# State @ w_in as float32r products of split parts, with later stores, a step on GpSimd and another order of the first steps

## The chip, the cores and the metric

One core of one Trainium2 chip runs the whole program. The metric is the device time of one execution in microseconds; of several runs of the same kernel the median counts. TensorE is called PE here, VectorE DVE, ScalarE ACT, GpSimd POOL and SyncE SP, as in the profile.

## What is computed

A small attention between tokens and a state (8 batches, 8 heads, 512 tokens, 32 state rows, head width 64) is followed by two feed-forward layers. All inputs and outputs are float32.

```python
scores = scale * (x @ state.T);  a  = softmax(scores);   xread = a @ state
scores2 = scale * (state @ x.T); a2 = softmax(scores2);  sread = a2 @ x
x = concat([xread, sread], axis=tokens)          # 8 x 544 rows of 512
h = x @ w_in                                     # 512 -> 2048
y = maximum(0.01 * h, h) @ w_out                 # 2048 -> 512
out = (silu(y @ w_gate) * (y @ w_val)) @ w_out2  # 512 -> 1536 -> 512
```

The weights arrive as pairs of 32-bit words (they are float64) and the kernel makes float32 numbers of them itself.

## The kernel before

**The three-pass product.** Where the kernel wants float32 accuracy it splits an operand into a high part (float32r, a cast on ACT, `split_h`, line 164) and a low part (the difference, on DVE, `split_l`, line 167), and multiplies low by high, high by low and high by high: three matmuls of 128x512 (`passes`, line 436). Nearly all of the program is made of these.

**State times w_in.** For the token rows xread is a @ state, so x @ w_in = a @ (state @ w_in). The kernel therefore forms state @ w_in (called sw) once, for each of four column groups g of w_in. This is done in two ways, both with plain float32 operands. `state_win` (line 453) makes what batch 0 needs, from a block layout `states` of the state, and keeps it on the chip; its two matmuls write 64 rows each. `product_sw` (line 462) makes the rows of four batches at once, for one pair of heads p: two matmuls, e = 0 and 1, one on partitions 0 to 63 and one on 64 to 127, into two PSUM banks. ACT copies both banks to a staging tile (line 474), and SP stores them to `sw_dram` (line 477), from where later batches load them (`load_sw`, line 504). There are 32 such products (4 groups, 4 pairs, 2 halves of the batches), listed in `products`; `pump_products` (line 1213) takes the next one whose weights are ready. Its banks are two of the y banks in the first steps, and a and b, always the same two, later. Five sets of staging tiles are used in turn (`stage_sw`, line 481).

**Making the weights.** `convert` (line 234) is a generator that a caller advances one quarter step at a time. For each 128x512 tile (a key) it issues on ACT a scale (line 214) and a conversion of the low word (line 215), and on DVE the sign (line 216), the limit (line 219, min and max against a constant), a join (line 222) and an add (line 225). Two keys are in work at a time, one behind the other, and the keys of w_out ("out") get their split into high and low parts a step after that. The 32 keys of the first layer are 16 of w_in ("in") and 16 of w_out, in the order of the string `ORDER`. The loads come on SP's queue (line 197) into five buffers; the finished w_in tiles are also stored to DRAM for later use (line 232), on the same queue.

**The order of the work.** It is written out by hand. `LOADS` orders the first DMAs. `START` is a string of letters for the first steps: c advances `convert` by a quarter of a key, p makes a product, 0 and 1 advance the attention of batch 0 (scores, softmax steps and splits, `read_state`, line 304) for its two quads of heads, h and l make and split a `state_win`, s and S lay out the state for the first and for the other batches, m makes the first h. The 16 strings of `SLOT0` then do the same for the 16 slots of batch 0: H makes h (six matmuls) for two slots later, Y and Z make y (two times six matmuls) from the activated h of this slot. Each engine gets its instructions in just this order and works them off in order. After batch 0 the later slots (1.36 us of h and 2.72 us of y each) have no products or weights of the first layer between them.

Of the kernel before, what the change touches and what calls it, by code (L numbers as in the profile page):

```python
# [25 lines left out]
def kernel(  # L26
# [38 lines left out]
    nc = tc.nc  # L65
# [25 lines left out]
    START = "spc0Scpccc0p0cpccpcc1ccchcc1cccpc1clcpp0hcccpclp1c01cpcmcc"  # L91
# [116 lines left out]
    def to_f32(key):  # L208
# [3 lines left out]
        v = raw[key].bitcast(I32)  # L212
        return {
# [5 lines left out]
            "limit": lambda: nc.vector.tensor_scalar(  # L219
# [14 lines left out]
    def convert(keys, room, prepare, load_next, finish=None):  # L234
# [4 lines left out]
        while todo or before or (finish and done):  # L239
# [209 lines left out]
    WO = {}  # L449
    products = []  # L450
    sw_ps, SW_raw, SW = {}, {}, {}
# [26 lines left out]

    sw_stages = []

    def stage_sw():

        if not sw_stages:
            y, x = ab.tile([P, KD, S], F32, tag="yst", name="sw"), first1.tile([P, 2, 512], F32, tag="x_tail", name="sw")
            sw_stages[:] = [[y[:, 0], y[:, 1]], [y[:, 2], y[:, 3]], [x[:, 0], x[:, 1]]] + [
# [18 lines left out]
    def load_sw(b, g, q):  # L504
        assert not any((g, p, b // 4) in products for p in (2 * q, 2 * q + 1))
        t = SW_raw[b, g, q] = xin.tile([P, 512], F32, tag="sw", name="sw")
# [525 lines left out]
    with tc.manual_schedule():  # L1032
# [15 lines left out]
        pair = [None]  # L1048

        def place1(key):  # L1050

            if key[0] == "in":
                n, half = divmod(KD * key[1] + key[2], 2)
                if half == 0:
# [438 lines left out]
```

## Time and profile before

| | |
|---|---|
| median of three runs | 1471.44 us (1468.38 to 1471.83) |
| the profiled execution: its own time | 1469.83 us |
| its span | 1468.0 us, 20651 instructions |
| busy: PE / DVE / ACT / POOL | 1444.3 / 829.5 / 687.8 / 3.0 us |
| DMA | 307.55 MB, mean 209 GB/s |

The span is cut into 40 slices on the page; the first four slices (some 147 us) hold the first steps and batch 0's slots, which is where the changed code runs. The granted clock stands at full speed in nearly all of the rest. A busy engine is one with an instruction in it; PE's matmuls overlap each other, so the distance from one start to the next is what a matmul costs.

### The profile page before, as it was taken

To read this page: it belongs to the slowest core of one execution; us is meant where nothing else is said; L and a number is where in the kernel's file an instruction comes from. 1 tells how busy PE (TensorE), PEld (TensorE's weight loads), DVE (VectorE), ACT (ScalarE), POOL (GpSimd) and SP (SyncE) were. 2 spreads that over 40 slices of the span, in tenths; PEclk is the share of its full clock that TensorE was granted. 3 is DMA by queue.
4 is the path that set the end of the run, shared out by engine and by line. 5 is a ranking of instruction groups with operands and counts; after the bars stand their busy time and mean duration, and the time that the engine had idled before them with its cause. 6 is when DMAs were issued, how large, how long until landed. Compare 5 with 4: busy or idle time off the path is not lost.

```text
span 1468.0 us, 20651 instructions
## 1 busy us (share of the span) xinstructions
PE 1444.3 (98%) x7530; PEld 1153.4 (79%) x7530; DVE 829.5 (57%) x1476; ACT 687.8 (47%) x1243; POOL 3.0 (0%) x8
## 2 busy tenths in 40 slices
PE   6999999999999999999999999999999999999998
PEld 1545777777777778888888888888888888988887
DVE  5877677677767676243454535555344655544442
ACT  6877656655655665454333433334233343333322
POOL 0000000000000000000000000000000000000000
PEclk8999999999999999999999999999999999999999
DMA  8895556665655656360668676667666397876345
GB/s 283 301 319 200 187 198 228 204 222 197 233 204 194 224 194 208 97 198 35 203 199 277 232 235 199 194 220 243 231 193 194 101 321 241 267 251 192 116 153 191
DMA packets 145764, 307.55 MB, mean 209 GB/s; under 512 B 14080, under 2 KB 34816, under 8 KB 144640
## 3 DMA queue, kind: packets, MB, share of 16 engines
q1 hardware_dynamic: 144368, 297.72, 61.7%
q10 hardware_dynamic: 1296, 8.52, 1.4%
q8 instruction: 60, 0.98, 0.3%
q14 instruction: 40, 0.33, 0.1%
HBM read 231.74 MB, written 74.45 MB: 209 GB/s over the span
## 4 chain that ended last, share of the span: by engine, by line
PE 97%; ACT 1%; DVE 1%; DMA 0%; issue 0%; SPq 0%; ACTq 0%
PE ps_y L444 24%; PE ps_o L444 19%; PE ps_x L742 18%; PE ps_h L444 14%; PE ps_s L742 9%; PE ps_a L742 4%; PE ps_sw L468 2%; PE ps_t L444 2%; PE ps_yt L444 2%; PE ps_s L319 1%; PE ps_r L416 1%; PE ps_sw L456 1%; PE ps_a L402 0%; ACT sw L474 0%; DMA flat<-in_dram 0%
## 5 line engine op out<-in xcount | busy, mean ns | idle before, releaser
L444 PE MATMUL ps_y<-gh,w_parts 128*128 128x512 f32 x1024 | 339.3, 391 | 0.0
L742 PE MATMUL ps_x<-yc,wq 128*128 128x512 f32 x1152 | 278.0, 389 | 0.0
L742 PEld LDWEIGHTS ps_x<-yc,wq 128*128 128x128 f32 x1152 | 216.2, 188 | 44.8
L444 PE MATMUL ps_o<-wo,zh 128*128 128x512 f32 x768 | 236.3, 389 | 0.0
L444 PEld LDWEIGHTS ps_y<-gh,w_parts 128*128 128x128 f32 x1024 | 192.2, 188 | 51.7 <-issue 7.6
L444 PE MATMUL ps_y<-gl,w_parts 128*128 128x512 f32 x512 | 199.4, 389 | 0.0
L168 DVE TENSOR_TENSOR gl<-hs,gh 128x512 fp32r<-128x512 f32 (+1 forms) x144 | 95.1, 661 | 141.6 <-ACT gh L165 141.4
L444 PEld LDWEIGHTS ps_o<-wo,zh 128*128 128x128 f32 x768 | 144.2, 188 | 29.8
L550 ACT ACTIVATE hs<-ps_h 128x512 f32<-128x512 f32 (+1 forms) x144 | 82.7, 574 | 172.4 <-PE ps_h L444 168.8
L444 PE MATMUL ps_o<-wo,zl 128*128 128x512 f32 x384 | 149.5, 389 | 0.1
L742 PE MATMUL ps_s<-yc,wq 128*128 128x512 f32 x576 | 146.1, 389 | 0.0
L168 DVE TENSOR_TENSOR zl<-z,zh 128x512 fp32r<-128x512 f32 x96 | 66.4, 691 | 114.6 <-ACT zh L165 114.6
L742 PEld LDWEIGHTS ps_s<-yc,wq 128*128 128x128 f32 x576 | 108.1, 188 | 22.4
L165 ACT CAST zh<-z 128x512 fp32r<-128x512 f32 x96 | 59.3, 622 | 140.7 <-PE ps_o L444 140.6
L762 ACT ACTIVATE sg<-C 128x512 f32<-128x512 f32 x72 | 45.5, 632 | 158.1 <-DVE C L758 158.1
L444 PEld LDWEIGHTS ps_y<-gl,w_parts 128*128 128x128 f32 x512 | 96.1, 188 | 19.6
L444 PE MATMUL ps_h<-ah,swl 128*128 128x512 f32 x256 | 106.3, 415 | 1.1 <-DVE swl L168 1.1
L758 DVE TENSOR_TENSOR C<-ps_s,C 128x512 f32<-128x512 f32 x48 | 33.2, 691 | 122.9 <-PE ps_s L742 122.9
L444 PE MATMUL ps_h<-al,swh 128*128 128x512 f32 x256 | 100.2, 391 | 0.2 <-DVE al L168 0.2
L754 ACT COPY C<-ps_x 128x512 f32<-128x512 f32 x96 | 55.9, 583 | 94.6 <-PE ps_x L742 94.6
L444 PE MATMUL ps_h<-ah,swh 128*128 128x512 f32 x256 | 100.2, 391 | 0.0
L165 ACT CAST gh<-hs 128x512 fp32r<-128x512 f32 (+1 forms) x144 | 85.7, 595 | 3.0
(129 smaller groups left out, 1912.8 us busy)
## 6 DMA issues: line engine op xcount, KB each, us to landing
wo<-wo SPq DMA_DIRECT2D x96, 512.0 KB
wq<-quad_gate SPq DMA_DIRECT2D x168, 256.0 KB
wq<-quad_val SPq DMA_DIRECT2D x168, 256.0 KB
ws<-in_dram SPq DMA_DIRECT2D x68, 512.0 KB
sw<-sw_dram SPq DMA_DIRECT2D x56, 256.0 KB
quad_gate<-hl SPq DMA_DIRECT2D x24, 512.0 KB
quad_val<-hl SPq DMA_DIRECT2D x24, 512.0 KB
yr<-y_dram SPq DMA_DIRECT2D x34, 256.0 KB
```

Source lines behind the costliest of these rows:

```text
L165: nc.scalar.copy(dst, src)
L168: nc.vector.tensor_tensor(out=dst, in0=src, in1=hi.bitcast(F32), op=ALU.subtract)
L319: nc.tensor.matmul(ps[2 * NS * i:2 * NS * (i + 1)], lhsT=states[:, p, b, :], rhs=xt.pop((b, p)), start=True, stop=True,)
L416: nc.tensor.matmul(ps[NS * k:NS * (k + 1), i], lhsT=v["et"][:, n:n + NS], rhs=tokens[i][:, c, NS * k:NS * (k + 1)], start=(c == 0), stop=( ...
L444: nc.tensor.matmul(ps, lhsT=w, rhs=v, start=first and n == 0, stop=last and n == len(todo) - 1)
L456: nc.tensor.matmul(ps[2 * NS * i:2 * NS * (i + 1)], lhsT=states[:, 2 * q + i, b, :], rhs=raw["in", g, 2 * q + i], start=True, stop=True,)
L468: nc.tensor.matmul(ps[e], lhsT=flat[half, p, 4 * bs:4 * bs + 4, :].rearrange("d b n -> d (b n)"), rhs=raw["in", g, p][half], start=True, s ...
L550: nc.scalar.activation(hs, ps[:, :n], AF.Prelu, alpha=0.01)
L742: nc.tensor.matmul(bank, lhsT=a, rhs=v, start=first and n == 0, stop=last and n == len(todo) - 1, skip_group_check=True,)
L754: nc.scalar.copy(t[0], src)
L758: nc.vector.tensor_tensor(out=kept[0], in0=bank, in1=kept[0], op=ALU.add)
L762: nc.scalar.activation(t[0], c, AF.Sigmoid)
```

## The change

- `product_sw` and `state_win` work on split parts: the state is split once (`flat_h`, `flat_l`, and for batch 0 a block layout `firsts_hl`), every w_in key is split like the w_out keys into a tile of `wres` (`finish1_h`, `finish1_l`), and three float32r passes take the place of one float32 product. `state_win` now multiplies full 128x128 blocks by `passes`, six matmuls instead of two. A w_in key is ready for products after its split, one step of `convert` later than before.
- the stores of a product are issued by `store_sw`, called when the next product is made (or before a load that needs them); there are four sets of staging tiles instead of five, and `flat` moves to another pool.
- `limit` runs on GpSimd for all keys but the first four.
- the layout of the state for batches 1 to 7 moves from ACT to GpSimd, which also fills `firsts_hl` by 16 small copies; ACT's table is loaded by a copy that waits for no DMA.
- `START` is rewritten: 28 quarter steps instead of 30, eight letters p instead of eleven (seven products are made ahead of the first y in both). `SLOT0` is as it was.

```diff
-    START = "spc0Scpccc0p0cpccpcc1ccchcc1cccpc1clcpp0hcccpclp1c01cpcmcc"
+    START = "sccccScc0ccc0cpccc10cpccpc1cpc0chc1chpc0lcp1l1mcpcpcc"
...
+        engine = nc.gpsimd if key[0] in ("in", "out") and key not in keys1[:4] else nc.vector
-            "limit": lambda: nc.vector.tensor_scalar(
+            "limit": lambda: engine.tensor_scalar(
...
-                if not finish or before[0] == "in":
+                store(before)
+                if not finish:
                     ready.append(before)
-                    store(before)
...
-    def state_win(b, g, q, bank):
+    def state_win(g, q, bank):
         ps = (ps_y if bank == "y" else ps_a).tile([P, 512], F32, tag=bank, name="ps_sw")
-        for i in range(2):
-            nc.tensor.matmul(
-                ps[2 * NS * i:2 * NS * (i + 1)], lhsT=states[:, 2 * q + i, b, :], rhs=raw["in", g, 2 * q + i],
-                start=True, stop=True,
-            )
+        passes(
+            [((first_h[:, 2 * q + i], first_l[:, 2 * q + i]), WIN[g, 2 * q + i]) for i in range(2)], ps, True, True
+        )
...
-        for e in range(2):
-            half = slice(D * e, D * (e + 1))
-            nc.tensor.matmul(
-                ps[e], lhsT=flat[half, p, 4 * bs:4 * bs + 4, :].rearrange("d b n -> d (b n)"),
-                rhs=raw["in", g, p][half], start=True, stop=True,
-            )
+        wh, wl = WIN[g, p]
+        for n, (st, w) in enumerate(((flat_l, wh), (flat_h, wl), (flat_h, wh))):
+            for e in range(2):
+                half = slice(D * e, D * (e + 1))
+                nc.tensor.matmul(
+                    ps[e], lhsT=st[half, p, 4 * bs:4 * bs + 4, :].rearrange("d b n -> d (b n)"), rhs=w[half],
+                    start=n == 0, stop=n == 2,
+                )
         staged = stage_sw()
         for e in range(2):
             nc.scalar.copy(staged[e], ps[e])
-            r = slice(NS, P) if bs == 0 else slice(0, P)
-            nc.sync.dma_start(out=sw_dram[bs][g][2 * p + e, r], in_=staged[e][r])
+        store_sw()
+        unstored.append((g, p, bs, staged))
...
         def finish1_h(key):
-            while any((KD * g + p) // 2 + NF1 // 2 == key[1] for g, p, _ in products):
-                pump_products(1)
-            t = wres.tile([P, 2, 512], F32R, tag=f"wr{key[1]}", name="w_parts")
+            place = key[1] if key[0] == "out" else places[KD * key[1] + key[2]]
+            clear(place)
+            t = wres.tile([P, 2, 512], F32R, tag=f"wr{place}", name="w_parts")
...
+        table = cv.tile([P, 1], F32, name="table")
+        nc.gpsimd.memset(table, 0.0)
+        nc.scalar.copy(table, table)
...
+        def split_states():
+            split_h(flat_h, flat)
+            split_l(flat_l, flat, flat_h)
+            for t, of in ((first_h, flat_h), (first_l, flat_l)):
+                for p in range(NPAIR):
+                    for e in range(2):
+                        half = slice(D * e, D * e + D)
+                        c = NS * (2 * (p % 2) + e)
+                        nc.gpsimd.tensor_copy(out=t[half, p, c:c + NS], in_=of[half, p, 0])
...
             elif action == "S":
-                place_states(slice(1, B))
+                split_states()
+                place_states(slice(1, B), nc.gpsimd.tensor_copy)
```

Three places show how this moves instructions. The first is PE in the first steps. Before, from the first scores (`ps_s`) to the first h (`ps_h`); `ps_sw<-w_in,flat` are products (x2 is one product), `ps_sw<-w_in,states` is a `state_win`:

```order
L319 MATMUL ps_s<-xt,states 64x512 x2
L468 MATMUL ps_sw<-w_in,flat 128x512 x2
L319 MATMUL ps_s<-xt,states 64x512 x2
L456 MATMUL ps_sw<-w_in,states 64x512 x2
L468 MATMUL ps_sw<-w_in,flat 128x512 x6
L456 MATMUL ps_sw<-w_in,states 64x512 x2
L468 MATMUL ps_sw<-w_in,flat 128x512 x6
L444 MATMUL ps_h<-ah,swl 128x512
```

Now, from the third product on (a product is two matmuls with `flat_l` and four with `flat_h`; `firsts_hl` x12 are both `state_win`):

```order
L474 MATMUL ps_sw<-w_parts,flat_l 128x512 x2
L474 MATMUL ps_sw<-w_parts,flat_h 128x512 x4
L446 MATMUL ps_sw<-w_parts,firsts_hl 128x512 x12
L474 MATMUL ps_sw<-w_parts,flat_l 128x512 x2
L474 MATMUL ps_sw<-w_parts,flat_h 128x512 x4
L474 MATMUL ps_sw<-w_parts,flat_l 128x512 x2
L474 MATMUL ps_sw<-w_parts,flat_h 128x512 x4
L446 MATMUL ps_h<-ah,swl 128x512
```

Seven products stood ahead of the first h; now five do, and the sixth and seventh stand between the first h and the second.

The second place is ACT a little before that first h. Before (214 and 215 are the scale and low-word steps of `convert`, `sw<-ps_sw` the copies of products, `ah` the splits of the two quads' softmax):

```order
L165 CAST ah<-a_298 128x512
L165 CAST swh<-ps_sw 128x512
L215 ACTIVATE ws<-ws 128x512
L474 COPY sw<-ps_sw 128x512 x2
L214 ACTIVATE ws<-ws 128x512
L165 CAST w_parts<-raw 128x512
L474 COPY sw<-ps_sw 128x512 x2
L165 CAST ah<-a_341 128x512
```

Now (216 and 217 are the same two steps):

```order
L165 CAST ah<-a_318 128x512
L165 CAST swh<-ps_sw 128x512
L216 ACTIVATE ws<-ws 128x512
L165 CAST w_parts<-raw 128x512
L346 ACTIVATE st<-st 128x512
L217 ACTIVATE ws<-ws 128x512
L165 CAST swh<-ps_sw 128x512
L480 COPY sw<-ps_sw 128x512 x2
L216 ACTIVATE ws<-ws 128x512
L165 CAST w_parts<-raw 128x512
L217 ACTIVATE ws<-ws 128x512
```

Casts of weight keys have come in, and the scale of the seventh key (the second 216) stands behind the cast of the second `state_win` and the copies of the fourth product.

The third place is DVE at the same time, from the steps that follow the first quad's softmax to the low split `al` of the second quad. Before:

```order
L168 TENSOR_TENSOR swl<-ps_sw,swh 128x512
L350 TENSOR_REDUCE r_336<-st 128x16
L351 TENSOR_SCALAR r_336<-r_336 128x16
L352 RECIPROCAL r_336<-r_336 128x16
L353 TENSOR_TENSOR st<-st,r_336 128x512
L355 STREAM_TRANSPOSE a_341<-st 128x512
L216 TENSOR_SCALAR w_in<-ws 128x512
L168 TENSOR_TENSOR al<-a_298,ah 128x512
L168 TENSOR_TENSOR al<-a_341,ah 128x512
```

Now:

```order
L168 TENSOR_TENSOR swl<-ps_sw,swh 128x512
L218 TENSOR_SCALAR raw<-ws 128x512
L352 TENSOR_REDUCE r_395<-st 128x16
L353 TENSOR_SCALAR r_395<-r_395 128x16
L354 RECIPROCAL r_395<-r_395 128x16
L355 TENSOR_TENSOR st<-st,r_395 128x512
L357 STREAM_TRANSPOSE a_400<-st 128x512
L168 TENSOR_TENSOR swl<-ps_sw,swh 128x512
L168 TENSOR_TENSOR al<-a_400,ah 128x512
```

The sign step of the seventh key (216, now 218), which reads what ACT's scale of that key wrote, has moved from behind the second quad's softmax steps to ahead of them.

## Rows read from the trace of the kernel before

**Rows 1.** The page, part 1: busy time, share of the span and instructions of each engine.

```profile
PE 1444.3 (98%) x7530; PEld 1153.4 (79%) x7530; DVE 829.5 (57%) x1476; ACT 687.8 (47%) x1243; POOL 3.0 (0%) x8
```

**Rows 2.** Stretches: length, busy PE, PEld, DVE, ACT, POOL (instructions), clock, DMA share, GB/s.

```profile
38.29:133.09 94.80, 90.25 (x336) 47.93 (x335) 77.42 (x147) 79.73 (x148) 0.00 (x0) 1.00 0.87 291
68.46:76.56 8.10, 8.10 (x31) 4.16 (x32) 7.63 (x16) 8.08 (x15) 0.00 (x0) 1.00 0.95 304
139.00:159.00 20.00, 20.00 (x90) 16.56 (x89) 6.29 (x11) 10.41 (x20) 0.00 (x0) 1.00 0.61 184
```

**Rows 3.** PE's waits, then ACT's, in 38 to 140 us: total, times, longest.

```profile
PE ps_sw L468 <- ACT sw L474: 3.5, 5, 0.8
...
ACT sw L474 <- PE ps_sw L468: 5.8, 12, 0.7
ACT swh L165 <- PE ps_sw L456: 5.1, 4, 2.1
...
ACT ws L214 <- DMA ws<-in_dram: 0.9, 2, 0.7
```

**Rows 4.** PE in order of time, one product between y and h: start, duration.

```profile
129.91 0.40 PE L444 MATMUL ps_y<-gh,w_parts 128*128 128x512 f32 x1
130.24 1.13 PE L468 MATMUL ps_sw<-w_in,flat 64*128 64x512 f32 x4
131.29 0.50 PE L444 MATMUL ps_h<-ah,swl 128*128 128x512 f32 x1
131.63 0.39 PE L444 MATMUL ps_h<-al,swh 128*128 128x512 f32 x1
131.86 0.39 PE L444 MATMUL ps_h<-ah,swh 128*128 128x512 f32 x1
```

**Rows 5.** The chain that ended last, two products in a row and a state_win: start, length.

```profile
110.77 1.11 PE ps_sw L468 x4
111.88 0.57 ACT sw L474
...
112.50 1.61 PE ps_sw L468 x3
...
117.05 1.01 PE ps_sw L456 x4
```

**Rows 6.** Groups of instructions of ACT and DVE, 0 to 140 us: busy, mean ns, idle before.

```profile
L474 ACT COPY sw<-ps_sw 128x512 f32<-128x512 f32 x64 | 34.5, 591 | 10.3 <-PE ps_sw L468 10.2
L165 ACT CAST w_parts<-raw 128x512 fp32r<-128x512 f32 x16 | 9.9, 618 | 0.0
...
L219 DVE TENSOR_SCALAR ws<-ws 128x512 f32<-128x512 f32 x32 | 13.5, 423 | 0.0
L168 DVE TENSOR_TENSOR w_parts<-raw,w_parts 128x512 fp32r<-128x512 f32 x16 | 10.9, 684 | 0.0
```

**Rows 7.** First steps: stretches (as rows 2), ACT in order of time, the chain.

```profile
7.80:20.00 12.20, 6.75 (x14) 1.52 (x12) 6.03 (x11) 7.33 (x13) 0.00 (x0) 0.72 0.66 238
20.00:36.00 16.00, 13.95 (x33) 4.38 (x31) 15.58 (x31) 11.71 (x22) 0.00 (x0) 0.79 0.95 328
28.00:32.00 4.00, 4.00 (x10) 0.81 (x9) 3.86 (x9) 2.58 (x5) 0.00 (x0) 0.50 1.00 356
...
4.85 1.28 ACT L1239 ACT_TABLE_LOAD   x1 [4.85 <-DMA flat<-in_dram]
10.27 1.88 ACT L1239 COPY states<-flat 64x896 f32<-64x896 f32 x2
...
37.51 3.51 PE ps_h L444 x14
```

**Rows 8.** Groups of POOL, whole span (as rows 6); SP's longest wait, 0:140.

```profile
L1350 POOL MEMSET zero<- 128x512 f32 x1 | 0.5, 526 | 548.9 <-PE ps_r L416 548.9
masks.py:199 POOL TENSOR_SCALAR_AFFINE_SELECT ident<-ident 128x128 f32<-128x128 f32 x1 | 0.3, 292 | 0.1
...
SPq L477 <- ACT sw L474: 35.2, 25, 3.8
```

More of the change, by code (lines that the diff above doesn't have):

```diff
@@ L449 @@
     WO = {}
+    WIN = {}
     products = []
+    kept = set()
     sw_ps, SW_raw, SW = {}, {}, {}
-    def state_win(b, g, q, bank):
+    def state_win(g, q, bank):
         ps = (ps_y if bank == "y" else ps_a).tile([P, 512], F32, tag=bank, name="ps_sw")
-        for i in range(2):
-            nc.tensor.matmul(
-                ps[2 * NS * i:2 * NS * (i + 1)], lhsT=states[:, 2 * q + i, b, :], rhs=raw["in", g, 2 * q + i],
-                start=True, stop=True,
-            )
+        passes(
+            [((first_h[:, 2 * q + i], first_l[:, 2 * q + i]), WIN[g, 2 * q + i]) for i in range(2)], ps, True, True
+        )
+        kept.add((g, q))
         return ps
@@ L505, in load_sw @@
         assert not any((g, p, b // 4) in products for p in (2 * q, 2 * q + 1))
+        if any((g, p, b // 4) == one[:3] for one in unstored for p in (2 * q, 2 * q + 1)):
+            store_sw()
         t = SW_raw[b, g, q] = xin.tile([P, 512], F32, tag="sw", name="sw")
@@ L1046, in next_load1, with clear, finish1_h @@
                 stage(key, src, cv)
-        pair = [None]
         def place1(key):
-            if key[0] == "in":
-                n, half = divmod(KD * key[1] + key[2], 2)
-                if half == 0:
-                    pair[0] = wres.tile([P, 2, 512], F32, tag=f"wr{n + NF1 // 2}", name="w_in")
-                raw[key] = pair[0][:, half, :]
-            else:
-                raw[key] = cv.tile([P, 512], F32, tag="raw", name="raw", bufs=4)
-        def finish1_h(key):
-            while any((KD * g + p) // 2 + NF1 // 2 == key[1] for g, p, _ in products):
-                pump_products(1)
-            t = wres.tile([P, 2, 512], F32R, tag=f"wr{key[1]}", name="w_parts")
-            WO[key[1]] = (t[:, 0, :], t[:, 1, :])
+            raw[key] = cv.tile([P, 512], F32, tag="raw", name="raw", bufs=4)
+        places = [*range(4, 16), *range(12, 16)]
+        holds = {}
+        def clear(place):
+            one = holds.pop(place, None)
+            while one and any((g, p) == one for g, p, _ in products):
+                pump_products(1)
+            assert not one or (one[0], one[1] // 2) in kept, one
+        def finish1_h(key):
+            place = key[1] if key[0] == "out" else places[KD * key[1] + key[2]]
+            clear(place)
+            t = wres.tile([P, 2, 512], F32R, tag=f"wr{place}", name="w_parts")
+            if key[0] == "in":
+                holds[place] = key[1:]
+            (WIN if key[0] == "in" else WO)[key[1:] if key[0] == "in" else key[1]] = (t[:, 0, :], t[:, 1, :])
             split_h(t[:, 0, :], raw[key])
         def finish1_l(key):
-            split_l(WO[key[1]][1], raw.pop(key), WO[key[1]][0])
+            parts = WIN[key[1:]] if key[0] == "in" else WO[key[1]]
+            split_l(parts[1], raw.pop(key), parts[0])
         keys2 = []
@@ L1221 @@
         low = list(keep)
-        flat = cv.tile([P, NPAIR, B, NS], F32, name="flat")
+        flat = ab.tile([P, NPAIR, B, NS], F32, tag="ah1", name="flat")
+        flat_h, flat_l = (cv.tile([P, NPAIR, B, NS], F32R, name=f"flat_{t}") for t in "hl")
+        firsts_hl = first1.tile([P, 2, NPAIR, P], F32R, tag="x_tail", name="firsts_hl")
+        first_h, first_l = firsts_hl[:, 0], firsts_hl[:, 1]
         for action in LOADS:
@@ L1232, with place_states @@
                 )
+        table = cv.tile([P, 1], F32, name="table")
+        nc.gpsimd.memset(table, 0.0)
+        nc.scalar.copy(table, table)
         nc.gpsimd.memset(states, 0.0)
+        nc.gpsimd.memset(firsts_hl.bitcast(F32), 0.0)
         make_identity(nc, ident)
-        def place_states(some):
+        def place_states(some, copy):
             for e in range(2):
                 half = slice(D * e, D * e + D)
-                nc.scalar.copy(states[half, :, some, NS * e:NS * e + NS], flat[half, :, some])
+                copy(states[half, :, some, NS * e:NS * e + NS], flat[half, :, some])
+        def split_states():
[3 more added lines that the diff above has]
+                for p in range(NPAIR):
+                    for e in range(2):
+                        half = slice(D * e, D * e + D)
+                        c = NS * (2 * (p % 2) + e)
+                        nc.gpsimd.tensor_copy(out=t[half, p, c:c + NS], in_=of[half, p, 0])
         background[0] = convert(keys1, lambda key: True, place1, next_load1, (finish1_h, finish1_l))
@@ L1253 @@
             elif action == "h":
-                keep_sw_h(*keep[0], state_win(0, *keep.pop(0), "y"))
+                pump_until(("in", keep[0][0], 2 * keep[0][1] + 1))
+                keep_sw_h(*keep[0], state_win(*keep.pop(0), "y"))
             elif action == "l":
@@ L1273 @@
             pump_until(("in", g, 2 * q + 1))
-            keep_sw_h(g, q, state_win(0, g, q, "y"))
+            keep_sw_h(g, q, state_win(g, q, "y"))
         for g, q in low:
@@ L1333 @@
             if i == NF1:
+                store_sw()
                 first.close()
```

15 lines of the change are left out of this document (10 added, 5 removed).

## The prediction

> **What bounds the kernel now.** I read the page's busy shares first: PE is busy for 98% of the span [rows 1]. Then the stretches: from 139 us on PE is busy without a gap, at full clock, with ACT and DVE at half load or below [rows 2]. Nothing in that part is changed, so whatever the changed part saves or loses by the last slot of batch 0 reaches the end one to one. All of the change lies in the first 140 us. Two stretches of them must be kept apart.
>
> The slots of batch 0, 38.29 to 133.09 us, take 94.80 us. PE is busy for 90.25 of them, DVE for 77.42, ACT for 79.73 with 148 instructions [rows 2], that is 0.54 us each. PE's waits there are few: 3.5 us for the copies of products [rows 3]. But the reader should look at ACT too: in the stretch from 68.46 it is busy for 8.08 of 8.10 us [rows 2], and where two products follow each other the chain leaves PE and goes over ACT's copy (1.11 us product, 0.57 copy, 1.61 second product [rows 5]). ACT in turn waits for PE: 5.8 us before copies and 5.1 before the casts of a `state_win` [rows 3]. So PE is the bound there, and ACT is close behind and tied to it. DMA is not: ACT waited 0.9 us for weights [rows 3], although the engines of the DMA are at 0.87 [rows 2].
>
> The first steps, up to 38 us, are bound by a chain through all engines. DVE is busy for 15.58 of the 16 us from 20 on, but only for 6.03 of the 12.20 before [rows 7]. PE's first unbroken run of h starts at 37.51 [rows 7].
>
> **The change, part by part.**
>
> *Products.* A float32 product costs 1.05 us: from its start at 130.24 to that of the next group at 131.29 [rows 4]. A float32r matmul costs 0.23 (131.63 to 131.86), the first of a group after a product 0.34 (131.29 to 131.63), and the last of a group before a product 0.33 (129.91 to 130.24) [rows 4]. No row shows float32r on half the rows of the array. If the two halves run side by side, as the four float32 records do (1.13 us for all four together [rows 4]), three passes cost 0.34 + 0.23 + 0.33 = 0.90, a gain of 0.15. If the halves came one after the other, six matmuls would cost 0.34 + 4 x 0.23 + 0.33 = 1.59, with the sixth in the last term, so a loss of 0.54. If the ends cost nothing, 0.69, a gain of 0.36. I take 0.15, since the two halves are the same tiles as before. Of 32 products 25 lie in the slots: -3.8 us, with ends of -9.0 and +13.5. The seven of the first steps are counted below, on their chain.
>
> *state_win.* It took 1.01 us [rows 5] plus a slower first matmul behind it (0.34 for 0.23 [rows 4]) and a slower last one ahead of it (0.33 for 0.23), 1.22 in all; six full matmuls are 6 x 0.23 = 1.38. Six lie in the slots: +1.0 (between 0.8 if the order around them saves less and 2.2 if those ends stay). PE alone would thus make the slots 2.8 us shorter: 92.0.
>
> *ACT.* The order of instructions gives 167 on ACT between the same two casts of h where 148 were: 13 more casts of weights, and 6 copies that stood in the first steps. 19 x 0.54 = 10.3, so ACT needs 90.0 of PE's 92.0 us. Nothing says it can't be 98% busy: from 68.46 it was [rows 2]. If all its waits for PE vanish, PE's 2.8 are gained in full; if only those before copies do and the 5.1 before the casts stay, the stretch is 90.0 + 5.1 = 95.1, or +0.3; if all 10.9 stay, 100.9, or +6.1. I take -1.3 for the slots, midway between the first two, because PE makes each product earlier and its copies are what ACT waited for most. The ends for the slots from PE and ACT together, without the unlikely halves in sequence: -5 and +6.
>
> *DVE and GpSimd.* In the slots 25 limits leave DVE (0.42 each [rows 6]: -10.6) and 12 low splits come (0.68 each [rows 6]: +8.2), so DVE falls from 77.4 to about 75. The trace has no limit on GpSimd. Its bounds from rows of GpSimd are 0.53 us, a memset of the same size that reads nothing, and 4 x 0.29 = 1.17, a select that reads and writes a quarter of it [rows 8]. I take 0 for the path at either end, because the limit of a key is needed only one key later, by the join, and a key takes four quarter steps. What would end that cover is a rival below.
>
> *The first steps.* Up to the second low split `al`, DVE gets the split of the state (twice 0.68) and four low splits (0.68 each), and loses two limits (0.42 each): +3.2. Its idle 6.2 us before 20 (12.20 - 6.03 [rows 7]) can take these, since ACT no longer spends 1.28 us on its table behind the state's load and 1.88 on laying out the state [rows 7], and the new `START` makes keys there. Against that stands the sign of the seventh key, now ahead of the second quad's softmax on DVE. It reads the scale that ACT issues behind the cast of the second `state_win` (1.38 us on PE and 0.6 on ACT) and two copies that need the fourth product (0.90, copies 2 x 0.54): DVE, which used to be full, stands still for about 2.2 us, or 4.4 if PE has the half clock that its row at 28 us shows (0.50 [rows 7]). `al` and the first h thus move by 3.2 - 6.2 + 2.2 = -0.8 to +1.4, and if only half of the early idle can be filled by 3 more. Behind the first h two products (2 x 0.90 = 1.8) now stand ahead of the second. Sum: +1.0 to +3.2, ends -1 and +6. I take +2, in the middle.
>
> *Stores and staging.* SP stood 35.2 us before stores whose copies were not done [rows 8], and loads of weights queue behind them. A product later these waits go. What they held up was late by at most the 0.9 us that ACT waited for weights [rows 3], so I cost the gain at nothing. The price is four staging sets instead of five: a set is reused after four products and stored one later, which leaves three, at 94.8 / 25 = 3.8 us each 11 us, for the store. Without that cover a copy waits for a store, and PE for the copy. The earlier readiness that w_in keys lose (one quarter-step cycle) I cost at nothing as well: what PE waits for most in the slots is copies, not a weight [rows 3].
>
> Sum: -1.3 + 2 = +0.7 on the profiled execution's 1469.8 us, 1470.5. That execution lies 1.6 us below the median of the runs shown, 1471.44. I forecast **1471.0 us**, no change that can be told: about 0.3%, 4.4 us, is what a measurement of this kernel can tell from none. The ends of this case alone are 1467 and 1475.5.
>
> **The rivals.**
>
> *ACT takes it all in, and the first steps aren't late.* The slots gain PE's 2.8 and the 3.5 that PE waited for copies [rows 3], 6.3 in all, and `START` comes out even at +0: 1469.8 - 6.3 = 1463.5. For it: the stretch with ACT at 8.08 of 8.10. Against it: the two products behind the first h.
>
> *ACT becomes the bound of the slots.* Its waits for PE (5.8 + 5.1 [rows 3]) stay beside its 90.0 us of work, 100.9, or +6.1; with the first steps at +2 the time is 1478. It decides once ACT keeps more than 94.8 - 90.0 = 4.8 us of its waits. For it: each engine works in order, so a cast put ahead of a copy delays the copy, and PE waits for that copy where products follow each other [rows 5]. Against it: the two stretches where ACT had no wait.
>
> *GpSimd and DVE get in each other's way.* If DVE stood still while a limit runs, its 75 us would grow by 25 x 0.53 = 13 or 25 x 1.17 = 29, to 88 or 104. It binds once a limit blocks for more than (92 - 75) / 25 = 0.68 us; at 1.17 the slots end 9 us late: 1481 with the first steps. The Trainium skill (SBUF — State Buffer, Who interferes with whom) says that a DVE instruction with two SBUF inputs contends with a GpSimd instruction that reads SBUF, and that the loser blocks fully. By that rule the joins, adds and low splits would all be hit; no row here has both engines at work, so the trace can't say. The Trainium skill (GPSIMD Engine Reference, Elementwise — side-by-side cycle accounting) has 0.77 us for 512 elements in its best loop, which no run here shows; by an estimate from it DVE would need 75 + 25 x 0.77 = 94 us, 2 more than PE.
>
> *The halves don't run side by side.* Then each product is dearer by 0.54 and the slots are 13.5 + 1.0 us longer on PE alone: 1486. The records of the float32 halves speak against it.
>
> **How the numbers follow.** The forecast has 0.45. The first rival has 0.30: ACT's full stretches make it credible. ACT as the bound has 0.14, the port 0.08, the halves 0.03. That gives faster by over 0.3% 0.30, within it 0.45, slower 0.25. The range reaches to 1463 for the first rival and to 1479 for the second; what it leaves out is the last two rivals and a corner of the first.
>
> **What would show it.** Right: products at 0.9 us from start to next group; the slots of batch 0 between 90 and 95 us, with ACT above 90% busy; the first unbroken run of h at 37 to 40 us and the second h two products later; the waits of SP for copies almost gone. Wrong: products at 1.6 us; DVE's joins and splits longer than 0.69 us or DVE waiting for GpSimd; ACT waiting for stores before a copy; or slots below 90 us, with PE's waits for copies gone.

## The result: slower by 1.3%

The changed kernel takes **1489.85 us** (median of 4 runs, 1489.28 to 1490.63), the kernel before 1471.34 (4 runs, 1468.38 to 1471.83). The ratio is 1.0133, 95% interval 1.0121 to 1.0145. That is 18.5 us more, outside the range of 1463 to 1479. The profiled execution of the changed kernel took 1490.63 us.

First the page, part 1, of the changed kernel; it answers to [rows 1]:

```profile
span 1488.8 us, 20950 instructions
...
PE 1452.9 (98%) x7610; PEld 1171.8 (79%) x7610; DVE 840.8 (56%) x1465; ACT 695.6 (47%) x1259; POOL 40.5 (3%) x56
```

These shares hide the loss. It is seen in the stretches of the changed kernel (columns as in [rows 2]): the slots of batch 0 between the same two h as there, then 20 to 40 us, five us behind a pause in the slots, and 20 us of the part that isn't changed.

```profile
40.55:155.68 115.13, 98.59 (x412) 62.60 (x412) 85.90 (x136) 89.91 (x167) 24.81 (x25) 0.94 0.73 245
20.00:40.00 20.00, 15.10 (x36) 7.80 (x35) 16.82 (x32) 11.66 (x22) 2.65 (x3) 0.50 0.74 235
122.00:127.00 5.00, 5.00 (x16) 3.66 (x14) 3.04 (x5) 2.73 (x5) 1.03 (x1) 0.61 1.02 338
160.00:180.00 20.00, 20.00 (x90) 16.53 (x90) 7.59 (x16) 11.24 (x21) 0.00 (x0) 1.00 0.36 115
```

From 160 us on PE is busy without a gap and at full clock, as it was. The slots took 94.80 us and take 115.13; the two products that now stand behind the first h lie in them, with 2.86 us (from 40.44 to 43.30). To compare both kernels up to a point where they run alike, here is the same stretch up to two h later, the kernel before and then the changed one:

```profile
38.29:144.72 106.43, 101.21 (x379) 55.43 (x378) 85.25 (x161) 85.68 (x159) 0.00 (x0) 1.00 0.83 278
```

```profile
40.55:165.01 124.46, 107.92 (x453) 70.04 (x454) 91.61 (x146) 94.36 (x176) 24.81 (x25) 0.94 0.70 234
```

So 18.0 us are lost here, and 2.3 ahead of it (the first h at 40.55 for 38.29): 20.3 of the 20.8 by which the span grew. Of the 18.0, PE is idle for 11.3 more (16.5 for 5.2) and busy for 6.7 more. The second part goes with the clock: it had been 1.00 throughout and is now 0.94 in the mean, near its lower level (0.61) behind a pause. An estimate of the busy time at full clock is 107.92 x 0.94 = 101.4, where the kernel before has 101.21. DMA is used less than before (0.70 for 0.83).

Who waits for whom in the changed kernel, 38 to 160 us (PE's and ACT's, DVE's; columns as in [rows 3]):

```profile
PE ps_sw L474 <- ACT sw L480: 10.2, 7, 3.5
DVE raw L218 <- ACT ws L216: 9.6, 6, 4.1
...
ACT sw L480 <- PE ps_sw L474: 8.0, 12, 2.6
ACT swh L165 <- PE ps_sw L446: 7.6, 4, 3.6
ACT w_parts L165 <- DVE raw L227: 7.2, 7, 1.8
```

PE's wait for the copies of products was 3.5 us and is 10.2. And there is a wait that the kernel before didn't have: ACT's cast of a key (L165) waits for DVE's add (L227). Four of these seven waits (3.6 us) are ahead of casts of w_in keys. Three (3.6 us) are ahead of casts of w_out keys, which the kernel before makes too, and without a wait for the add. The largest pause, with PE's half clock behind it, reads as follows: DVE, then ACT, then PE, each in order of time (start, duration, idle before):

```profile
115.95 0.70 DVE L335 STREAM_TRANSPOSE st<-s 128x512 f32<-128x512 f32 x1
116.69 0.69 DVE L336 TENSOR_REDUCE m<-st 128x16 f32<-128x512 f32 x1
117.29 0.68 DVE L224 SCALAR_TENSOR_TENSOR raw<-ws,raw 128x512 int32<-128x512 int32 x1
117.89 0.69 DVE L168 TENSOR_TENSOR w_parts<-raw,w_parts 128x512 fp32r<-128x512 f32 x1
118.49 0.69 DVE L227 CUSTOM_DVE_ANT_0 raw<-ws,raw 128x1024 uint16<-128x1024 uint16 x1
```

```profile
117.02 0.67 ACT L216 ACTIVATE ws<-ws 128x512 f32<-128x512 f32 x1
119.21 0.62 ACT L165 CAST w_parts<-raw 128x512 fp32r<-128x512 f32 x1 [1.52 <-DVE raw L227]
119.73 1.06 ACT L480 COPY sw<-ps_sw 128x512 f32<-128x512 f32 x2
```

```profile
115.88 0.50 PE L474 MATMUL ps_sw<-w_parts,flat_l 64*128 64x512 f32 x2
116.22 0.62 PE L474 MATMUL ps_sw<-w_parts,flat_h 64*128 64x512 f32 x4
120.37 1.28 PE L474 MATMUL ps_sw<-w_parts,flat_l 64*128 64x512 f32 x2 [3.52 <-ACT sw L480]
...
122.43 0.79 PE L446 MATMUL ps_y<-gh,w_parts 128*128 128x512 f32 x1
```

The product at 115.88 was done at 116.8. Its copies stand on ACT behind the cast of a key (one of w_out), the cast waits for the add of that key, and the add stands on DVE behind two softmax steps, a join and the low split of the key before. That one is a w_in key, so this low split is part of the change. The copies come at 119.73, and the second product starts at 120.37, when the first of the banks is free. PE stood for 3.52 us, and the next y's matmul takes 0.79 instead of 0.50.

### The profile page after: what moved, and what is told of

It is laid out like the page before. It is cut to its first block, busy times and chain, and to the rows that moved or that the text cites. A ratio compares the mean times of both kernels' runs of the same rounds, so it can differ in the third digit from the quotient of the medians.

```text
span 1488.8 us, 20950 instructions
## 1 busy us (share of the span) xinstructions
PE 1452.9 (98%) x7610; PEld 1171.8 (79%) x7610; DVE 840.8 (56%) x1465; ACT 695.6 (47%) x1259; POOL 40.5 (3%) x56
## 4 chain that ended last, share of the span: by engine, by line
PE 91%; DMA 3%; DVE 2%; ACT 2%; issue 1%; SPq 0%; POOL 0%; ACTq 0%; POOLq 0%
PE ps_y L446 22%; PE ps_o L446 18%; PE ps_x L758 18%; PE ps_h L446 13%; PE ps_s L758 9%; PE ps_a L758 4%; PE ps_t L446 2%; PE ps_yt L446 2%; DMA ws<-in_dram 1%; PE ps_s L321 1%; PE ps_sw L474 1%; DMA sw_dram<-sw 1%; PE ps_r L418 1%; ACT sw L480 1%; DMA sw<-sw_dram 1%
## 5 line engine op out<-in xcount | busy, mean ns | idle before, releaser
L165 ACT CAST zh<-z 128x512 fp32r<-128x512 f32 x96 | 59.3, 622 | 141.5 <-PE ps_o L446 141.4
L165 ACT CAST gh<-hs 128x512 fp32r<-128x512 f32 (+1 forms) x144 | 85.7, 595 | 3.0
```

Of the source, the lines that this page charges most:

```text
L165: nc.scalar.copy(dst, src)
```

## The experiments

Five theories stood at first: **1**, GpSimd's limit and DVE hold each other up; **2**, the cast behind its own add; **3**, the first steps; **4**, the later stores; **5**, the later readiness of the w_in keys. Three were added on the way: **6**, DVE's low split; **7**, the work of both halves of the split, in the written order of two engines; **8**, PE's need of the fresh halves. Each result is the ratio to the kernel before, measured on the same chip, with its interval; 0.1% are 1.5 us. The changed kernel itself has 1.0133 (1.0121 to 1.0145).

### One part of the change undone

**limit_on_dve:** `engine = nc.vector` in `to_f32`.

> The changed kernel with one part undone: the limit of the w_in and w_out keys stands on DVE again. Theory 1 (the GpSimd limit and DVE's low split of the weights hold each other up, the adds come late, and ACT's casts and copies with them): DVE takes 28 limits of about 0.42 us back (+11.8 us of work) and loses the 32 x 0.29 = 9.4 us by which its low splits were stretched; the w_parts low split reads 0.65 to 0.70 us instead of 0.98, and most of the 14.9 us lost in the slots of batch 0 comes back: 1476 to 1482 us. Theory 2 (ACT waits because the cast of a key now stands right behind its own add, whoever does the limit): ACT w_parts still waits about 10 us for DVE's add, 1487 to 1493. Theory 3 (the 5.4 us of the first steps and their half clock): those are untouched, 1488 to 1491. Theory 4 (stores a product later) likewise 1488 to 1491.

1487.24 us, 1.0119 (1.0104 to 1.0134). The collisions go, as these groups show (0 to 162 us: busy, mean ns, idle before; the changed kernel, then this one):

```profile
L168 DVE TENSOR_TENSOR w_parts<-raw,w_parts 128x512 fp32r<-128x512 f32 x32 | 31.3, 977 | 3.4 <-ACT w_parts L165 3.4
...
L221 POOL TENSOR_SCALAR ws<-ws 128x512 f32<-128x512 f32 x28 | 27.5, 981 | 100.5 <-DVE raw L218 80.0 <-ACT sw L480 8.9 <-DMA sw_dram<-sw 4.1
...
L165 ACT CAST w_parts<-raw 128x512 fp32r<-128x512 f32 x32 | 19.9, 623 | 9.9 <-DVE raw L227 9.9
```

```profile
L168 DVE TENSOR_TENSOR w_parts<-raw,w_parts 128x512 fp32r<-128x512 f32 x32 | 21.9, 686 | 3.4 <-ACT w_parts L165 3.4
...
L165 ACT CAST w_parts<-raw 128x512 fp32r<-128x512 f32 x32 | 19.9, 622 | 7.7 <-DVE raw L227 7.6
...
L221 DVE TENSOR_SCALAR ws<-ws 128x512 f32<-128x512 f32 x32 | 13.6, 425 | 0.0
```

The low split falls from 977 to 686 ns, 9.4 us of DVE's time, while 11.9 us of limits come back to DVE; from the first h to the sixteenth DVE is busy for about as long (91.08 us, 91.61 in the changed kernel). The time moves by 0.14%, and the intervals overlap. Theory 1 isn't the cause of the loss.

**stores_at_once:** in `product_sw` the call of `store_sw()` stands behind `unstored.append(...)`.

> The changed kernel with one part undone: each product's two stores are issued right behind its copies again. Theory 4 (the later stores delay the rows of sw_dram and the loads behind them): 3 to 6 us faster, 1484 to 1487. Theories 1 to 3: SP waits a little longer for ACT's copies, with 11 us or more between a store and its load as cover: 1488 to 1492.

1490.13 us, 1.0137 (1.0122 to 1.0152): theory 4 falls. The later stores are worth nothing either way.

**old_start:** the `START` of the kernel before.

> The changed kernel with the order of the first steps of the kernel before. Theory 3 (the new order puts two products at half clock between the first and the second h, and with it ACT's copies ahead of the conversion: first y at 47.45 us where it was 42.01): first y at 42 to 44 us, 3 to 6 us faster, 1484 to 1487. Rival (the first steps are late because of the work added ahead of them, the split states, their copies and 8 more conversion instructions, in whatever order): first y at 46 us or later, 1488 to 1492, or slower, if products that now wait for split keys stand in the way.

1489.80 us, 1.0138 (1.0123 to 1.0153). The first y stands at 50.32 us, later than the 47.45 of the changed kernel, since the old order asks for a `state_win` and products before their keys are split (PE waits 5.3 us there for casts and low splits of keys). So this run doesn't take the delay back, and the order alone isn't shown to cost anything here.

**products_ahead_of_h:**

```diff
-    START = "sccccScc0ccc0cpccc10cpccpc1cpc0chc1chpc0lcp1l1mcpcpcc"
+    START = "sccccScc0ccc0cpccc10cpccpc1cpc0chc1chpc0lcp1l1cpcpmcc"
```

> The changed kernel with two products of the first steps moved ahead of the first h instead of behind it. Theory 3: PE waits 1.5 to 2 us there for the split of the first attention anyway, the second h comes 2 to 3 us earlier (43.30 us in the changed kernel) and the end too: 1486.5 to 1488. Rival: ACT's four copies now stand ahead of what the first h waits for, and nothing is gained: 1489 to 1491.

1489.86 us, 1.0127 (1.0106 to 1.0147): the rival. The first y comes at 46.62 instead of 47.45, and the slots give it back.

### One part of the change alone, in the kernel before

**before_limit_pool:** the choice of the engine for the limit, put into `to_f32` of the kernel before.

> The kernel before with one part of the change alone: the limit of all keys of layer 1 but the first four on GpSimd. Theory 1: the low splits of w_out there (L168, 0.68 us) are stretched to about 1.1 us where a limit overlaps, adds come late and products or casts behind them: 4 to 10 us slower, 1475 to 1481. Theory 2 (the limit costs little; what costs is the cast of the w_in keys, which this kernel doesn't have): within 2 us of 1471.4. Theories 3 and 4 as theory 2.

1471.76 us, 1.0015 (1.0005 to 1.0024). The 16 low splits of w_out are stretched to 962 ns there too (684 in [rows 6]), and 2.2 us is all that comes of it.

**before_late_keys:** in `convert`, for a w_in key, `ready.append` moves from the add to the place where the next step's low split stands.

> The kernel before with one thing of the change alone: a w_in key counts as ready three quarters of a conversion step later, as it does once it has a split; no work is added, and its products stay float32. Theory 5 (readiness: products and state products are pushed back, and the conversion is pumped ahead of them): 3 to 8 us slower, 1473 to 1478, with longer gaps ahead of ps_sw and a later first h. Theories 1 to 3 (it is the work itself: GpSimd's port, ACT's casts, the order of the first steps): within 2 us of 1470.

1471.91 us, 1.0011 (1.0000 to 1.0021). Theory 5 is worth 1.6 us here, and 3 at the upper end of the interval.

### Where the split is made

**cast_later:**

```diff
-            if split:
-                finish[0](done)
             if prev:
                 prev["limit"]()
             yield 0.42
             if key:
                 ops["low"]()
                 ops["sign"]()
+            if split:
+                finish[0](done)
```

> The changed kernel with one line moved: in the conversion ACT's cast of a finished key stands behind the low-word activation of the next key instead of ahead of it, a quarter of a step later, so that it no longer stands right behind its own add. Theory 2: the 9.9 us that ACT waits for DVE's add fall to under 3, the copies of the products come earlier, 5 to 10 us faster: 1480 to 1485. Theory 1: the add is as late as before and the wait is only moved (to DVE's low split, which waits for the cast, or to the next products): 1486 to 1492. Theories 3 and 4: 1488 to 1491.

1484.96 us, 1.0106 (1.0089 to 1.0124): the best of what can be done with one line, about a fifth of the loss, with the upper end of its interval still touching that of the changed kernel. ACT's wait for the add shrinks, as expected (1.4 us are left in 40 to 140 us), but DVE's low split now waits for the cast (5.1 us in the same stretch).

**cast_on_pool:** limit on DVE, and in `finish1_h` `nc.gpsimd.tensor_copy` for the w_in keys.

> The changed kernel with the limit on DVE (1487.2 us) and the high-part cast of the w_in keys on GpSimd instead of ACT: no work is left out. Theory 2 and its wider form (ACT, in its own order, holds the copies of products behind casts that wait, and 16 x 0.62 = 9.9 us of casts are added to it): 5 to 10 us faster than 1487.2, with PE ps_sw behind ACT sw at under 5 us. Theory 6 (DVE): within 3 us of 1487.2. Theory 1 (GpSimd in DVE's way, and a GpSimd cast of about 1 us ahead of the low split): 0 to 5 us slower than 1487.2.

1491.85 us, 1.0150 (1.0134 to 1.0165). It is slower than limit_on_dve, whose interval only touches this one. The cast takes 875 ns on GpSimd for 623 on ACT:

```profile
L1086 POOL CAST w_parts<-raw 128x512 fp32r<-128x512 f32 x15 | 13.1, 875 | 90.9 <-DVE raw L227 80.3 <-PE ps_sw L474 10.6
```

The loss against limit_on_dve lies in the first steps: the first h comes at 42.23 us, for 39.16 there. From it to the sixteenth h this kernel takes 121.93 us and limit_on_dve 122.63, although ACT has 6.7 us less to do; PE's wait for copies is 7.4 us for 9.3. Taking the cast from ACT thus gives the slots next to nothing, but since the cast is longer on GpSimd the run doesn't rule theory 2 out.

### The split left out

**no_low_w_in:** `finish1_l` does nothing for w_in, and `WIN`'s high part stands for the low one.

> The changed kernel without DVE's low split of the 16 w_in keys: this leaves out the low parts of w_in, each pass on them takes the high part instead, so the matmuls stay as many. Theory 6 (DVE's added work sets the slots of batch 0: 16 low splits of 0.68 us, 0.98 as measured, delay every add behind them): 8 to 14 us faster, 1476 to 1482. Theory 2 (ACT's cast behind the add): the add that follows a low split comes 0.7 to 1.1 us earlier, which takes some of the 9.9 us of ACT's wait: 3 to 6 us faster. Theory 3 or 5: within 2 us of 1489.9.

1485.47 us, 1.0108 (1.0093 to 1.0123).

**no_cast_w_in:** `WIN[key[1:]] = (first_h, t[:, 1, :])`, with no cast.

> The changed kernel without ACT's cast of the 16 w_in keys alone: the products take the small split states in SBUF for the high part of w_in, which leaves that part out; DVE's low split stays, as long as before. Theory 2 in its wide form (ACT's added work and its wait, 16 x 0.62 us and 9.9 us, carry the loss): 10 to 14 us faster than the changed kernel, 1476 to 1480, as without the whole split. Theory 7 (each half costs about its own length, only both together give 14 us): without the low part it was 4.4 us, so 6 to 9.5 us faster here, 1480 to 1484. Theory 6 (DVE): under 4 us faster, 1486 or more.

1488.51 us, 1.0116 (1.0100 to 1.0133). The low split stands here as before, but takes the small state from the key and so doesn't wait for a cast; its result carries the part of w_in that the expectation says is left out. Either half alone thus gives back some 0.2%, with intervals that overlap that of the changed kernel. The prediction of theory 7 for this run, that each half costs about its own length, was wrong.

**no_split_w_in:** `WIN[key[1:]] = (first_h, first_l)`, and neither half is made.

> The changed kernel without either half of the split of the 16 w_in keys (ACT's cast and DVE's low split, 0.62 and 0.68 us each): this leaves w_in out of the products, which multiply the small split states that lie in SBUF anyway; the matmuls, copies, stores, the keys' late readiness, the limit on GpSimd and the order of the steps stay. Theory 7 (no single engine: ACT and DVE take turns in their written order, each waits for the other, and 16 x (0.62 + 0.68) = 20.8 us of split work put into that chain lengthen it by most of their sum): 13 to 20 us faster, 1470 to 1477. Theory 6 (DVE's part alone): as without the low split, 1484 to 1487. Theory 5 or 3 (late readiness, first steps): 1484 to 1490.

1476.06 us, 1.0033 (1.0024 to 1.0042). Both halves together give back 1.0%, three quarters of the loss, and more than twice the sum of the halves. The stretch from the first h to the sixteenth shows where the excess comes from (without the low split, without the cast, without both; the changed kernel's is the line with 124.46 above; all four have 453 matmuls):

```profile
37.97:160.60 122.63, 110.08 (x453) 72.38 (x454) 84.52 (x134) 94.39 (x176) 24.86 (x25) 0.92 0.71 238
```

```profile
40.25:162.68 122.43, 109.34 (x453) 71.67 (x454) 91.57 (x146) 88.00 (x163) 24.77 (x25) 0.92 0.70 238
```

```profile
35.04:149.96 114.92, 105.13 (x453) 69.77 (x454) 84.23 (x134) 88.20 (x164) 24.84 (x25) 0.95 0.75 254
```

PE's idle time is 16.5 us in the changed kernel and 12.6, 13.1 and 9.8 here. In it the halves nearly add: 4.0 and 3.5 alone, 6.8 together. The excess lies in PE's busy time, which with one half gone is 2.2 and 1.4 us longer at a clock of 0.92, and with both gone 2.8 shorter at 0.95, and in the first h, which comes 2.6, 0.3 and 5.5 us earlier. These are single executions; those with one half took 2.8 and 0.9 us more than their medians.

**no_split_w_in_early:** the same, with `ready.append(before)` behind the add for w_in.

> As no_split_w_in, and a w_in key counts as ready right behind its add, as in the kernel before; w_in is left out of the products likewise. Theory 5 (readiness): 3 to 6 us faster than no_split_w_in. Theory 7: within 2 us of it. Beside the kernel before it then differs by the limit on GpSimd, the stores, the first steps and the three-pass products: what is left of the 18.5 us is theirs, by theory 3 some 5 us (1474 to 1477), by theory 7 under 3 us (1469 to 1473).

1475.56 us, 1.0032 (1.0022 to 1.0042): readiness costs nothing here.

**no_split_early_old_start:** the same with the `START` of the kernel before.

> As no_split_w_in_early (1475.6 us: no w_in split, w_in left out of the products, keys ready as in the kernel before), and the order of the first steps of the kernel before. Theory 3 for what remains (the new order of the first steps costs about 5 us once nothing else hides it): 1469 to 1472, with the second h at 2 us behind the first. Rival (the state split and its small copies, the three-pass products and their copies, whatever the order): 1474 to 1477.

1470.96 us, 1.0003 (0.9994 to 1.0012). The remaining 0.3% are the new order of the first steps, which counts once the split no longer hides it. This kernel has the three-pass products, GpSimd's limit and the later stores, lacks the split of w_in, and is as fast as the kernel before, not faster.

### Work or dependency

Without the split the products depend on nothing fresh. So the last two runs make both halves and use them in no product.

**split_unused:** as no_split_w_in, but `split_h` and `split_l` are issued at their places into the key's own tile.

> The changed kernel with both halves of the w_in split made as they are there, and used by no product: the products take the small split states in SBUF, which leaves w_in out of them. Theory 7 (the work itself, 16 x (0.62 + 0.68) us in ACT's and DVE's written order): within 3 us of the changed kernel, 1486 to 1491. Theory 8 (the dependency: a product can't start before the cast and the low split of a key that was made ready just ahead of it): as without the split, 1475 to 1479.

1485.97 us, 1.0116 (1.0101 to 1.0131).

**split_unused_early_old_start:** the same work put back into no_split_early_old_start.

> no_split_early_old_start (1470.96 us) with both halves of the w_in split put back, used by no product. Theory 7: 8 to 14 us slower than that, 1479 to 1485. Theory 8: within 2 us of it, 1469 to 1473. Between the two (1473 to 1479): the late readiness and the order of the first steps, which this kernel has from the kernel before, are part of what the work costs in the changed kernel.

1485.62 us, 1.0107 (1.0090 to 1.0124). Against the same kernel without the work (1.0003) that is 1.04%, 15.3 us; in the other pair (1.0116 against 1.0033) it is 0.83%, 12.2 us. Theory 8 falls, theory 7 stands: **the work costs the time, even where no product needs it.** What the order and the readiness add doesn't show once the work is there.

The two traces show the same pattern as before and after the change. The stretch from the first h to the sixteenth, no_split_early_old_start and then split_unused_early_old_start:

```profile
40.40:148.70 108.30, 101.70 (x441) 67.65 (x440) 83.89 (x135) 85.10 (x159) 24.53 (x25) 0.97 0.80 269
```

```profile
42.20:161.05 118.85, 105.74 (x441) 70.15 (x440) 90.76 (x147) 91.91 (x172) 24.53 (x25) 0.93 0.75 245
```

The matmuls are the same 441. ACT has 13 and DVE 12 instructions more, 6.8 and 6.9 us of work each, and the stretch is 10.6 longer: PE is idle for 6.5 more and, at the lower clock, busy for 4.0 more. (The profiled execution of the first kernel took 1475.29 us, 4.3 above its median.) And the waits of the first kernel, then of the second (38 to 160 us):

```profile
PE ps_sw L478 <- ACT sw L484: 4.3, 6, 1.1
```

```profile
PE ps_sw L477 <- ACT sw L483: 9.0, 6, 3.1
...
ACT w_parts L165 <- DVE raw L227: 4.6, 6, 1.8
```

PE waits as often for a copy, six times, but twice as long, and the cast's wait for the add is back.

### Looking for something better

**three_together:** cast_later, limit on DVE and the `START` of products_ahead_of_h.

> The changed kernel with the cast moved a quarter step later (alone: -4.6 us), the limit on DVE (alone: -2.2) and the two products ahead of the first h. If these costs add: 1480 to 1483. If they are the same wait seen from two engines (theory 7: whatever is taken from one, the next one in the chain takes over): 1484 to 1487.

1485.25 us, 1.0092 (1.0070 to 1.0115). cast_later alone has 1.0106, well within this interval. The sum of the three gains measured alone (0.27, 0.14 and 0.06%) would be 1.0086, which lies in it as well, so this run can't tell whether the remedies add.

**keep_later:** `KEEP = (0, 1, 3, 5, 8, 9)`, the last 7 before.

> The changed kernel with one state product (group 3, second half) two slots later, where its key is ready without three quarter steps of conversion forced in ahead of it. Theory 5 in the slot where it can be seen (the slot that begins at 116.54 us takes 14.05 us, 8.87 in the kernel before; without the split it still takes 13.4 us with late keys and 10.7 with early ones): that slot falls to 10 to 11.5 us and the end comes 2 to 4 us earlier, 1486 to 1488. Rival (the conversion has to be done anyway, by the same slots): the time goes to the next slots, 1489 to 1491.

1496.11 us, 1.0172 (1.0157 to 1.0187). Neither theory expected a loss. The state product now stands just ahead of the h that needs its low split (PE, 145 to 152 us; start, duration):

```profile
145.09 2.71 PE L446 MATMUL ps_sw<-w_parts,firsts_hl 128*128 128x512 f32 x6 [0.94 <-ACT sw L480]
...
151.21 0.50 PE L446 MATMUL ps_h<-ah,swl 128*128 128x512 f32 x1 [2.20 <-DVE swl L168]
```

**cast_keep_limit:** cast_later, limit on DVE and keep_later in one.

> The changed kernel with the cast a quarter step later (alone -4.6 us), the limit on DVE (alone -2.2 us) and the state product of keep_later. Theory 7: these take out waits but not the 20.8 us of split work: 1481 to 1484, above the kernel before. If late readiness and the cast's place were all: 1474 or less.

1487.65 us, 1.0115 (1.0100 to 1.0130): no faster than cast_later alone; whether the loss of keep_later is in it the intervals don't tell. No version was found below the kernel before. That no_split_early_old_start, with no split at all, only equals it speaks against looking further along this line.

## Why the prediction was wrong

**The step that failed is the term for ACT in the slots.** Its count was right: 167 instructions and 90.0 us of work were foretold, 167 and 89.91 were measured. What was wrong is "I take -1.3 for the slots", which let the new work fill ACT's waits for PE. Its main ground was a stretch of 8.10 us in which ACT had no wait. The waits grew instead: before copies from 5.8 to 8.0 us, before the casts of a `state_win` from 5.1 to 7.6, and 7.2 new ones for DVE's add. In the slots ACT's work grew by 10.2 us and its idle time by as much again (15.1 to 25.2). Slots that were to take 93.5 took 115.13, or some 112 without the two products that the prediction counts with the first steps. That the split of w_in, on ACT and DVE together, causes most of the loss is shown by the runs with and without it: 12.2 and 15.3 us. The rival "ACT becomes the bound" named the mechanism (a cast put ahead of a copy delays the copy, and PE waits for that copy), but its price of +6.1 was a limit that didn't hold, because it let the old waits at most stay and left out the wait of the cast itself. The clock is a second term that the sum didn't have: PE's 92.0 us were taken at full clock, as [rows 2] has it, and what was granted is 0.94 in the mean.

- **Products** were right: from the start of one at 46.55 to the next group 0.90 us (rows below). The halves run side by side: two records of 0.49 us each take 0.50 together. That PE needs less didn't reach the end, not even without the split (1.0003). The rule for it is in the Trainium skill (TensorEngine Tiling (Array Packing), PSUM Bottleneck): tiling speeds TensorE up but not the emptying of PSUM, whose copies may become the bottleneck. By it the 3.8 us weren't to be counted on; the trace agrees, with 64 copies of 590 ns as before (591 in [rows 6]) and 10.2 us of PE waiting for them, though in the pause shown above it is the cast ahead of the copies that holds them.
- **DVE and GpSimd** at nothing on the path: nearly right for the limit. It took 981 ns, within the bounds of 0.53 and 1.17. It blocks, as the third rival said, but not for its whole length, as that rival's sum had it: the low splits grew by 9.4 us over 28 limits, 0.34 each and below the 0.68 from which it was to bind. Its removal gave 0.14%. But DVE was to fall to about 75 us in the slots and was busy for 85.90, since what the limits left free the stretched low splits took back; and its low splits of w_in at no price on the path are half of the work that the runs show to cost the time.
- **First steps** at +2: the first h was 2.3 us late, but the first y 5.4 (47.45 for 42.01). The two products behind the first h took 2.86 us and not 1.8, since the clock was at its lower level (0.50 from 20 to 40 us). Those 5.4 don't show as a separate item in the changed kernel: with the first y at 46.62 (products_ahead_of_h) nothing was gained, and the old order made it later still (50.32). Without the split the old order gave 0.3%.
- **Stores and readiness** at nothing: right, by stores_at_once and before_late_keys. That SP's waits for copies would almost vanish was wrong: 18.4 us for 35.2. Beside them stand 28.9 of waits for adds, ahead of the stores of w_in (0 to 140 us); all waits ahead of those stores were some 26 us before and are some 47 now:

```profile
SPq L234 <- DVE raw L227: 28.9, 10, 4.3
SPq L493 <- ACT sw L480: 18.4, 13, 4.7
```

The product at 46.55 and the first matmul behind it:

```profile
46.55 0.50 PE L474 MATMUL ps_sw<-w_parts,flat_l 64*128 64x512 f32 x2
46.89 0.63 PE L474 MATMUL ps_sw<-w_parts,flat_h 64*128 64x512 f32 x4
47.45 0.51 PE L446 MATMUL ps_y<-gh,w_parts 128*128 128x512 f32 x1
```

**Open:** both halves together cost four to six times what either gives back alone. PE's idle time doesn't show this excess; its clock and the first steps do. Why the clock stayed at 0.92 with one half gone, although PE stood less, no run tells. The chain that ended last names DMA for some pieces of 3 to 9 us in the slots; nothing here took a DMA away, though at 0.70 of its engines' time and with the stores moved at no effect it isn't likely.

## What to carry to other kernels

Where engines work in a written order and wait for each other at every step, free time on one of them is not room: without the split ACT and DVE were busy for nearly 80% of the slots, and 7 us more on each made the stretch 11 us longer. Before work is put in such a gap, follow what stands behind it on its engine, and what it waits for, up to the engine that sets the end. A faster product gave nothing here, not even where no split was in the way; and a pause on PE was paid a second time where the clock was granted at its lower level behind it (3.52 us of pause, then 0.61 over five us).

## What the hardware showed

The limit takes 0.65 us on GpSimd where DVE is idle (from 45.55 to 46.69), and 1.02 where DVE reads two inputs beside it; DVE's low split is stretched with it (GpSimd, then DVE, of the changed kernel):

```profile
45.63 0.65 POOL L221 TENSOR_SCALAR ws<-ws 128x512 f32<-128x512 f32 x1 [9.58 <-DVE raw L218]
...
58.70 1.02 POOL L221 TENSOR_SCALAR ws<-ws 128x512 f32<-128x512 f32 x1 [3.50 <-DVE raw L218]
```

```profile
58.53 0.69 DVE L224 SCALAR_TENSOR_TENSOR raw<-ws,raw 128x512 int32<-128x512 int32 x1
59.13 1.13 DVE L168 TENSOR_TENSOR w_parts<-raw,w_parts 128x512 fp32r<-128x512 f32 x1
60.18 0.68 DVE L227 CUSTOM_DVE_ANT_0 raw<-ws,raw 128x1024 uint16<-128x1024 uint16 x1
```

The join that began ahead of the limit kept its 0.69 us, and the limit was late; the low split that began while the limit ran took 1.13; the add behind it is whole again. This agrees with the Trainium skill (SBUF — State Buffer, Who interferes with whom): the one that issues first has the shared port, the other is held up. For DVE the move of the limit was thus no relief, 11.9 us of limits for 9.4 of stretched low splits, and the whole moved by 0.14 to 0.15% only. The surprises were the small gain (0.25%) of taking 16 low splits of 0.68 us from DVE, and the 0.4%, 6 us, that one state product in a wrong place cost.
